# A searched order with new durations, constant products ahead of eight chunks, and loads held behind one matmul

## The chip, the cores and the metric

The kernel runs on one core of a Trainium2 chip. The metric is the device time of one execution in microseconds (us). The profile was taken of one further execution; its engines are named as on the page: PE (TensorE matmul), PEld (its weight loads), DVE (VectorE), ACT (ScalarE), POOL (GpSimd) and SP (SyncE, which here issues most DMAs).

## The reference

One block of a network on x of 2048 x 640 (all float32). A vector c gives six rows by silu(c) @ w_mod: sa, ca, ga, sb, cb, gb.

```python
x = A_u
h = layernorm(x) * (1 + ca) + sa
x = x + ga * A(h)          # S4D: a causal convolution along the sequence
h = layernorm(x) * (1 + cb) + sb
x = x + gb * B(h)          # SwiGLU: (silu(h @ w1) * (h @ w3)) @ w2

def A(u):                  # per channel d of 640, with N = 128 states
    P = exp((A * dt)[:, :, None] * arange(2048))
    K = 2 * einsum("dn,dnl->dl", C * dt, P).real
    return irfft(rfft(u, 4096) * rfft(K, 4096))[:2048] + u * D_skip
```

B has F = 1728 hidden channels.

## The kernel before

**Convolution.** The 640 channels are worked in five blocks (`NB`) of 128. For each block b three streams of work meet:

- *The kernel K* (`gen_tasks`, `gen_chunk`, from L566). Each block has 8 chunks of 16 channels, 40 in all. A chunk is: on POOL a phase table `ph` and three magnitude products (two into `yy`, one into `xx`); on ACT the sines into `tr`; on DVE five products into `yy` and `xx`; then on PE `product()` (L604): 32 small matmuls (128 x 32 by 128 x 64) that sum over the 128 states into `kps`, one half of a PSUM bank. ACT copies `kps` to `ks` (`rows`), and DVE adds the skip term (`skip`). `ph`, `xx`, `yy` and the halves of the bank `kg` are rings of two.
- *The normed input h* (`h_tasks`). Four quarters per block: load `xq` (for block 0 into `sp`), normalise into `hn` (`h_norm`, L990: four instructions of 128 x 128, on ACT or on DVE), multiply and add rows (`hn`, `hb`), store to DRAM `hs`, fetch as `xb`.
- *The spectra* (`first_tasks`, `spectra_tasks`). A transform in two steps: `ps` (PE, with the constant `wk`; from `xb` for h, from `ks` for K), copied into `sp` by ACT or DVE; then `fh` and `fk` (PE, with the constant `wb`), the complex product `fp` (DVE, from `hz` and `fk`), the first inverse step `fz` (PE, with the constant `wz`), copied to `zt` and stored to DRAM `zd`.

Before these, block 0 needs the parameters, the statistics of x (`xs`, `hscale`), and the modulation rows: `pm` (five groups of four products side by side, as the five pieces of `w_mod` land), `m`, `prow`, `rw`, `fold`; a second half of `w_mod` gives `cols`.

**What sets the order.** `Plan` (L172) lists all these tasks with an engine or a choice of engines, a duration, what each waits for, and the rings that it takes from and gives to. `place` walks through them, picks at each step the ready task by its start and its rank, and assigns the engine where there is a choice (`h_norm`, the copies of `ps` and `fz`, `al8`, `mag`). The ranks come from the long list `RANKS` (L33). The result is the program order on each engine (`Engines`, `InOrder`, L148: each instruction is ordered behind the one before it on its engine). All these instructions have L157 in the profile. SP's DMAs are in that order too; a DMA waits in SP until what it needs is there, and those behind it wait with it.

**Border.** When the last chunk of K and the last `hn` are done, `change` (L907) frees the tables and SP loads the first 512 rows of x (`x2[0]`), the constant `wd` (1 MB), and, as tasks, the first two weight tiles of the FFN and the first units of the second inverse step: `iz` (loaded from `zd`, without the last block's 128 columns) and `iy` (PE, with `wd`), which DVE adds to `x2`. After `plan.run()` (L946) the plan is over. Then come, written out in `run` (from L950): `izb` (L956), the last block's 128 columns of the first 512 rows, in four pieces of 128 KB (two issued by SP, two by ACT), which need the last `zd` store; `inverse` on them; `ln2` (L669: LayerNorm, `xn`, twenty transposes `tp` by PE, `v`, and the halves `xh` and `xl`); and the FFN. In this part the order on an engine is set by the scheduler and by priorities, and nothing but data holds a load back. Only `load_x2(1, last)` (L960) is given a wait for the last `izb` matmul.

**FFN.** `ffn` (L755) has four row blocks of 512 and 14 tiles of F. A tile is `up` (gu, L796 to L798, three matmuls per product since every factor is split into a high and a low half), `gate`, `down` (acc, L833). Tiles 0 and 13 of row block 0 were loaded and split ahead. While row block 0 runs, `mid` (L962) brings in the other 1536 rows' convolution: `inverse_unit(u)` for u = 2 to 7 loads `iz` (four pieces of 320 KB) and runs `iy` (L654); `load_x2(2)` and `load_x2(3)` load the rest of x. `x2[b]` is four loads of 320 KB. The first `iy` of the FFN (unit 2) stands on PE behind the first two tiles' gu.

Of the kernel before, what the change touches and what calls it, by code (L numbers as in the profile page):

```python
# [10 lines left out]
F32 = mybir.dt.float32  # L11
# [7 lines left out]
P = 128  # L19
# [263 lines left out]
class K:  # L283
# [282 lines left out]
    def gen_chunk(self, d0, tabs, off, E, place):  # L566
# [36 lines left out]

        def product():  # L604
            kps = place()
            for e in range(C // 4):
                for q in range(4):
                    i = e * 4 + q
                    for r in range(2):
# [938 lines left out]
```

## Time and profile before

| | |
|---|---|
| time, median of 3 | 1003.81 us (1002.39 to 1005.65) |
| profiled execution, its own time | 1003.62 us |
| its span | 1001.8 us |
| mean granted PE clock | 0.964 |
| busy: PE, DVE, ACT, POOL | 885.9, 667.6, 496.7, 287.4 us |
| moved by DMA | 122.03 MB, 122 GB/s on average |

The span reaches from the first to the last of the program's own instructions; the execution's time is 1.8 us longer. In the table of 40 slices, one slice is 25 us. PEclk is the clock that TensorE was granted, in tenths of full speed. A row of the timeline gives start and length of a run of like instructions on one engine, and in brackets how long the engine had been idle before it and what ended that. A float32 product is two records on PE, so x8 is four products. A row of busy time by stretch gives, after its length, busy us and number of instructions for PE, PEld, DVE, ACT and POOL, then the granted clock, the share of 16 DMA engines and GB/s. A row of a group by line gives busy time and mean ns, then idle time before it.

### The profile page before, as it was taken

How to read it: one execution, taken by the hardware profiler on the slowest of the kernel's cores; microseconds unless marked ns; L12 is line 12 of the kernel's file. 1: busy time of each engine (PE TensorE's matmuls, PEld its weight loads, DVE VectorE, ACT ScalarE, POOL GpSimd, SP SyncE). 2: the span in 40 equal slices, each digit the busy share in tenths (PEclk: the TensorE clock that was granted, in tenths of full speed). 3: DMA queues.
4: the chain of work that ended last, by engine and by line, in shares of the span. 5: the costliest groups of instructions: out<-in, count | busy, mean ns of one | idle time of the engine just before them, and what ended most of it. 6: DMA issues, size and time to landing. Idle time of an engine off the chain costs nothing.

```text
span 1001.8 us, 20149 instructions
## 1 busy us (share of the span) xinstructions
PE 885.9 (88%) x8073; PEld 706.8 (71%) x8073; DVE 667.6 (67%) x1234; ACT 496.7 (50%) x829; POOL 287.4 (29%) x293
## 2 busy tenths in 40 slices
PE   1464877889999992999999999999999999999997
PEld 1142766767887961677788888888888888888885
DVE  7998999999999573677664454463644544645442
ACT  6867787979787731432243242342333332433221
POOL 1798798989999230100000000000000000000000
PEclk9976998999999995999999999999999999999999
DMA  9954553624041398967132353233453323542301
GB/s 218 267 187 169 123 131 103 150 56 117 24 107 45 90 280 221 225 160 178 56 114 70 105 152 112 79 90 94 106 145 99 99 79 93 145 118 79 105 27 52
DMA packets 141189, 122.03 MB, mean 122 GB/s; under 512 B 13480, under 2 KB 124840, under 8 KB 139688
## 3 DMA queue, kind: packets, MB, share of 16 engines
q1 hardware_dynamic: 140360, 119.84, 44.5%
q8 instruction: 63, 1.03, 0.4%
q10 hardware_dynamic: 736, 0.92, 0.3%
q14 instruction: 30, 0.25, 0.1%
HBM read 99.75 MB, written 20.97 MB: 121 GB/s over the span
## 4 chain that ended last, share of the span: by engine, by line
PE 72%; DVE 13%; DMA 8%; ACT 3%; issue 3%; SPq 0%; ACTq 0%; DVEq 0%
PE acc L833 19%; PE gu L798 12%; PE gu L797 12%; PE gu L796 12%; PE ps L157 4%; DVE yy L157 3%; PE kps L157 2%; PE fk L157 2%; PE fz L157 2%; PE fh L157 2%; DVE xx L157 2%; DMA sp<-in_w_mod 2%; DVE fp L157 2%; DMA zd<-zt 2%; DVE hn L157 2%
## 5 line engine op out<-in xcount | busy, mean ns | idle before, releaser
L798 PE MATMUL gu<-xh,wl 128*128 128x512 f32 x540 | 212.9, 394 | 0.0
L797 PE MATMUL gu<-xl,wh 128*128 128x512 f32 x540 | 211.6, 392 | 0.0
L796 PE MATMUL gu<-xh,wh 128*128 128x512 f32 x540 | 210.7, 392 | 0.1
L732 ACT ACTIVATE wh<-wr 128x640 fp32r<-128x640 f32 x105 | 71.8, 731 | 136.0 <-PE gu L797 132.8
L744 POOL MEMSET w2l<- 64x640 f32 x3 | 1.9, 630 | 450.8 <-PE acc L833 450.8
L797 PEld LDWEIGHTS gu<-xl,wh 128*128 128x128 f32 x540 | 101.5, 188 | 23.6
L796 PEld LDWEIGHTS gu<-xh,wh 128*128 128x128 f32 x540 | 101.6, 188 | 22.8 <-ACT xh L666 0.5
L798 PEld LDWEIGHTS gu<-xh,wl 128*128 128x128 f32 x540 | 101.4, 188 | 21.4
L809 ACT ACTIVATE th<-gu 128x512 f32<-128x512 f32 x52 | 31.2, 599 | 130.7 <-PE gu L798 130.6
L811 DVE TENSOR_TENSOR a<-a,gu 128x512 f32<-128x512 f32 x52 | 35.7, 687 | 88.2 <-PE gu L798 88.1
L157 POOL TENSOR_TENSOR yy<-e,e 128x512 f32<-128x512 f32 x80 | 86.3, 1096 | 16.7 <-PE kps L157 11.9
L833 PE MATMUL acc<-w2l,ah 128*128 128x512 f32 x220 | 87.0, 396 | 0.0
L833 PE MATMUL acc<-w2h,ah 128*128 128x512 f32 x220 | 87.0, 395 | 0.0
L810 DVE SCALAR_TENSOR_TENSOR a<-th,gu 128x512 f32<-128x512 f32 x52 | 35.7, 687 | 76.5 <-ACT th L809 76.4
L733 ACT ACTIVATE w2h<-w2r 128x640 fp32r<-128x640 f32 x54 | 39.9, 738 | 94.2 <-issue 56.6
L745 DVE TENSOR_TENSOR w2l<-w2r,w2h 128x640 fp32r<-128x640 f32 (+1 forms) x54 | 44.4, 822 | 57.9 <-ACT w2h L733 57.8
L741 DVE TENSOR_TENSOR wl<-wr,wh 128x640 fp32r<-128x640 f32 x105 | 82.4, 818 | 0.0
L157 POOL TENSOR_TENSOR ph<-p,p 128x1024 int32<-128x1024 int32 x40 | 79.1, 1978 | 5.5 <-ACT tr L157 4.7
L833 PE MATMUL acc<-w2h,al 128*128 128x512 f32 x204 | 77.6, 395 | 0.0
L157 DVE TENSOR_TENSOR yy<-yy,tr 128x512 f32<-128x512 f32 (+1 forms) x80 | 75.4, 944 | 0.9 <-ACT tr L157 0.6
L157 PE MATMUL kps<-yy,xx 128*32 128x64 f32 x2560 | 51.5, 236 | 26.0 <-DVE xx L157 20.0
L157 PEld LDWEIGHTS kps<-yy,xx 128*32 128x32 f32 x2560 | 45.1, 117 | 35.9 <-issue 19.9
(229 smaller groups left out, 1688.0 us busy)
## 6 DMA issues: line engine op xcount, KB each, us to landing
wr<-in_w SPq DMA_DIRECT2D x104, 320.0 KB, 3.8
w2r<-in_w SPq DMA_DIRECT2D x52, 320.0 KB, 2.8
zd<-zt SPq DMA_DIRECT2D x39, 256.0 KB, 2.8
iz<-zd SPq DMA_DIRECT2D x24, 320.0 KB, 6.2
xs<-in_x SPq DMA_DIRECT2D x16, 320.0 KB, 11.4
hs<-hb SPq DMA_DIRECT2D x20, 256.0 KB, 2.4
xb<-hs SPq DMA_DIRECT2D x20, 256.0 KB, 4.4
x<-in_x SPq DMA_DIRECT2D x16, 320.0 KB, 5.6
```

The costliest lines, as they stand in the source:

```text
L157: self.prev = self.k.order(f(*a, **kw), self.prev)
L732: self.nc.scalar.activation(wh[:, i], raw[:, i], AF.Copy)
L733: self.nc.scalar.activation(w2h, w2r, AF.Copy)
L741: eng.tensor_tensor(wl[:, i], raw[:, i], wh[:, i].bitcast(F32), op=ALU.subtract)
L745: eng.tensor_tensor(w2l[q], w2r[q], w2h[q].bitcast(F32), op=ALU.subtract)
L796: nc.tensor.matmul(pg, wh[:, k, :], xh[:, k, :], start=(k == 0), stop=False)
L797: nc.tensor.matmul(pg, wh[:, k, :], xl[:, k, :], start=False, stop=False)
L798: nc.tensor.matmul(pg, wl[:, k, :], xh[:, k, :], start=False, stop=(k == KT - 1))
L809: nc.scalar.activation(th, gu[0], AF.Tanh, scale=0.5)
L810: nc.vector.scalar_tensor_tensor(a, th, 1.0, gu[0], op0=ALU.add, op1=ALU.mult)
L811: nc.vector.tensor_mul(a, a, gu[1])
L833: nc.tensor.matmul(acc[k], *two(a, w), start=(m == 0 and i == 0), stop=(m == 12 and i == 2))
```

## The change

Four things change.

1. The list `RANKS` is another one, and three durations and one wait that the plan reckons with are others: `h_norm` on DVE 1.75 instead of 0.85, `fold` 3.3 instead of 1.6, one more entry (400000 bytes) for the first loads, and in block 0 each `product` also waits for `wk`. So the order and the choice of engines of the whole convolution are new; it has the same tasks.
2. In block 0 each of the eight `product()` groups is preceded on PE by four products of the identity with the constant `wk` (128 x 256), into the same half bank, which the group then overwrites.
3. At the border, `awake` puts products of the identity with `wd` (128 x 512) into a bank that is not read: eight behind the last planned matmul, three behind the last `izb` matmul.
4. `held_back` makes every `load_x2` after the first and every `inverse_load` after `izb` wait for the last `izb` matmul.

The diff without the ranks:

```diff
         def product():
             kps = place()
+            if d0 < P:
+                for _ in range(4):
+                    nc.tensor.matmul(kps, self.ident, self.wk.rearrange("p a b -> p (a b)"), start=True, stop=True)
...
-    def load_x2(self, b, after=None):
+    def load_x2(self, b):
         for q in range(4):
-            i = self.nc.sync.dma_start(self.x2[b][q * 32:(q + 1) * 32], self.xv[q, :, 4 * b:4 * b + 4, :])
-            if after is not None:
-                self.tc.add_manual_dep(i.ins, after.ins.name, ...)
+            self.held_back(self.nc.sync.dma_start(self.x2[b][q * 32:(q + 1) * 32], self.xv[q, :, 4 * b:4 * b + 4, :]))
...
-                (other if g and other else self.nc.sync).dma_start(z[pr][g * 64:(g + 1) * 64], zv[:, t0:t0 + nj, d0:d1])
+                self.held_back((other if g and other else self.nc.sync).dma_start(z[pr][g * 64:(g + 1) * 64], zv[:, t0:t0 + nj, d0:d1]))
...
+    hold = None
...
         plan.run()
-        self.nc = nc = real
+        self.nc = real
...
-        z = self.inverse_load("izb", ip, "izb", 1, 0, 4, cut, D, nc.scalar)
-        last = self.inverse(0, 4, z, ps, "gu", 3, cut, D)
+        z = self.inverse_load("izb", ip, "izb", 1, 0, 4, cut, D, real.scalar)
+        self.awake(nc.tensor, po.tile([P, 512], F32, name="awake0", tag="acc4"), 8)
+        self.hold = nc.tensor.prev = self.inverse(0, 4, z, ps, "gu", 3, cut, D)
+        self.awake(nc.tensor, po.tile([P, 512], F32, name="awake1", tag="acc4"), 3)
...
-        self.load_x2(1, last)
+        self.load_x2(1)
...
-            add(n + "p", "PE", 1.1, lambda c=c: ch[c][4](), [n + f"m{i}" for i in range(5)], t + 3,
+            add(n + "p", "PE", 1.1, lambda c=c: ch[c][4](), [n + f"m{i}" for i in range(5)] + ([] if b else ["wk"]), t + 3,
...
-            add(n + "n", ("ACT", "DVE"), (1.95, .85), ...
+            add(n + "n", ("ACT", "DVE"), (1.95, 1.75), ...
...
-        add("ld", "SP", 0, None, [], next(lp), dma=[2560, 327680, 2560])
+        add("ld", "SP", 0, None, [], next(lp), dma=[2560, 327680, 2560, 400000])
...
-        add("fold", "DVE", 1.6, fold, ...
+        add("fold", "DVE", 3.3, fold, ...
...
+    def held_back(self, i):
+        if self.hold is not None:
+            self.tc.add_manual_dep(i.ins, self.hold.ins.name, mybir.DependencyInfo(mybir.DependencyClass.Sync, mybir.DependencyReason.DATA), reason="behind")
+
+    def awake(self, pe, to, n):
+        v = self.wd.rearrange("p a b c -> p (a b c)")[:, :512]
+        for i in range(n):
+            pe.matmul(to, self.ident, v, start=True, stop=True)
```

More of the change, by code (lines that the diff above doesn't have):

```diff
@@ L628, in pbank @@
         return self.psg.tile([P, 512], F32, name=name, tag="f", bufs=3)
-    def load_x2(self, b, after=None):
+    def load_x2(self, b):
         for q in range(4):
-            i = self.nc.sync.dma_start(self.x2[b][q * 32:(q + 1) * 32], self.xv[q, :, 4 * b:4 * b + 4, :])
-            if after is not None:
-                self.tc.add_manual_dep(i.ins, after.ins.name, mybir.DependencyInfo(mybir.DependencyClass.Sync, mybir.DependencyReason.DATA), reason="behind")
+            self.held_back(self.nc.sync.dma_start(self.x2[b][q * 32:(q + 1) * 32], self.xv[q, :, 4 * b:4 * b + 4, :]))
     def inverse_load(self, name, pool, tag, bufs, j0, nj, d0, d1, other=None):
@@ L1154, in h_tasks @@
             place = (lambda: self.pbank("hn")) if b else (lambda: self.psg.tile([P, 512], F32, name="hn", tag="f", bufs=3))
-            add(n + "n", ("ACT", "DVE"), (1.95, .85), lambda e, i=i, place=place: self.h_norm(b, i, place(), e), [n + "l", "hscale"], t, take=[(bank, 1)],
+            add(n + "n", ("ACT", "DVE"), (1.95, 1.75), lambda e, i=i, place=place: self.h_norm(b, i, place(), e), [n + "l", "hscale"], t, take=[(bank, 1)],
                 give=[("xq", n + "l")] if b else [])
@@ L1472, in fold @@
             V.tensor_mul(self.rB, self.rB, self.rows[2])
-        add("fold", "DVE", 1.6, fold, [f"rw{g}" for g in range(4)], 22, port=True)
+        add("fold", "DVE", 3.3, fold, [f"rw{g}" for g in range(4)], 22, port=True)
         add("wb", "SP", 0, lambda: nc.sync.dma_start(self.wb, self.t_wb), ["fold", "mr4", "lat1", "turn1"], 60, dma=[2097152])
```

130 rows, old and new, of the table RANKS are left out of this document.

## The prediction

> **What bounds the kernel now.** I read the page's slices first, then busy time by stretch of 25 us, then the stretch around 375 to 415 us by engine.
>
> ```profile
> span 1001.8 us, 20149 instructions
> ...
> PE   1464877889999992999999999999999999999997
> ...
> DVE  7998999999999573677664454463644544645442
> ...
> PEclk9976998999999995999999999999999999999999
> ```
>
> The right 24 slices are the FFN: PE is never idle there, at full clock. The left 15 are the convolution, where DVE is at nine tenths or more. Between them, in slice 16 (375 to 400 us), PE drops to 2 tenths and its clock to half. A gain can come from two places only: the convolution ends earlier, or the hole gets shorter. The FFN's instructions stay as they are, some 596 us from 405 to the end.
>
> ```profile
> core 0: us, PE busy (x) PEld busy (x) DVE busy (x) ACT busy (x) POOL busy (x), PEclk, DMA share, GB/s
> ...
> 50.00:75.00 25.00, 16.07 (x276) 10.07 (x280) 24.24 (x53) 17.26 (x36) 23.23 (x24) 0.77 0.55 185
> 75.00:100.00 25.00, 10.17 (x241) 6.53 (x232) 20.64 (x33) 19.85 (x31) 20.68 (x22) 0.69 0.49 170
> ...
> 275.00:300.00 25.00, 24.70 (x546) 21.12 (x544) 24.65 (x43) 22.31 (x40) 24.28 (x24) 1.00 0.45 108
> ...
> 325.00:350.00 25.00, 25.00 (x524) 22.39 (x522) 14.91 (x27) 17.87 (x32) 7.05 (x6) 1.00 0.34 85
> ```
>
> In the convolution DVE has almost no air (24.2 and 24.7 of 25), except in 75 to 100; POOL has 1 to 4 us in a stretch, ACT 3 to 8. From 275 on PE is full as well. So less DVE work helps early, and only as far as it lets PE do more before 275.
>
> The hole, on all engines:
>
> ```profile
> 375.38 1.94 PE L157 MATMUL iy<-iz,wd 128*64 128x512 f32 x8
> 386.66 1.54 PE L654 MATMUL iy<-izb,wd 128*64 128x128 f32 x6 [9.34 <-DMA izb<-zd]
> 392.12 1.94 PE L654 MATMUL iy<-izb,wd 128*64 128x128 f32 x10 [3.92 <-DMA izb<-zd]
> 399.41 4.53 PE L691 MATMUL tp<-ident,xn 128*128 128x128 f32 x20 [5.35 <-ACT xn L682]
> 404.04 1.20 PE L796 MATMUL gu<-xh,wh 128*128 128x512 f32 x3
> ```
>
> ```profile
> 383.25 1.25 SPq L644 DMA_DIRECT2D izb<-zd  x2
> 384.54 2.18 SPq L632 DMA_DIRECT2D x<-in_x  x4
> 386.78 0.48 SPq L644 DMA_DIRECT2D iz<-zd  x1
> 394.08 2.33 SPq L632 DMA_DIRECT2D x<-in_x  x4
> 396.46 4.96 SPq L644 DMA_DIRECT2D iz<-zd  x7
> ```
>
> ```profile
> 383.96 8.02 DMA izb<-zd
> ```
>
> ```profile
> DMA to landing us min/median/max: 2.8/4.6/8.0
> ```
>
> PE ends its planned work at 377.3. The last z store lands at 383.25, four izb pieces of 128 KB are issued (two by SP, two by ACT), and the last, issued by ACT at 383.96, takes 8.02 us, to 391.98: five loads of 320 KB were put into SP's queue right behind izb. Then come the matmuls, LayerNorm and twenty transposes, until gu starts at 404.04.
>
> **The change, part by part.** All against the profiled execution, 1003.62 us (span 1001.8 and 1.8 around it), 0.2 below the median 1003.81.
>
> *Loads held back.* In the built program of the changed kernel SP issues izb and then x21, x22, iz2, iz3, x23, the first of them waiting for the last izb matmul. Nothing runs beside izb any more. Its last piece then takes between 2.8 and 8.0 us; I take 4.0, near the median 4.6 and a little below, since that median holds pieces already in the crowd. 8.0 - 4.0 = **-4.0 us** (0 to -5.2).
>
> *The price of holding back.* iz2 was partly ahead (one piece at 386.78). Now, counted from the last izb matmul, it stands behind eight pieces of x21 and x22, and is the ninth to twelfth of 320 KB. The next weights stand behind x23, further from their use.
>
> ```profile
> 386.60:392.10 5.50, 1.54 (x6) 1.15 (x7) 0.00 (x0) 0.00 (x0) 0.00 (x0) 0.50 1.02 229
> ```
>
> ```profile
> 414.89 0.83 PE L654 MATMUL iy<-iz,wd 128*64 128x320 f32 x4
> ```
>
> At 229 GB/s a piece (327,680 bytes) takes 1.43 us, twelve 17.2; with some 2.3 us of latency (the quickest landing of 128 KB above, 2.8, less its own share of 0.6) the twelfth lands about 19.5 us behind. PE used iz2 414.89 - 394.06 = 20.8 us behind, and will want it 1.7 us sooner by the next term, at 19.1. I take **+0.7 us** (0 to +3); it is partly covered by the wait for the gate that stands behind those matmuls anyway.
>
> *Products of constants at the border.* Eight of 128x512 stand behind the last planned matmul, three behind the last izb matmul.
>
> ```profile
> 59.78 1.77 PE L157 MATMUL prow<-m,ident 128*128 128x512 f32 x4
> ...
> 73.05 1.96 PE L157 MATMUL kps<-yy,xx 128*32 128x64 f32 x64
> ...
> 79.35 1.16 PE L157 MATMUL kps<-yy,xx 128*32 128x64 f32 x64 [1.51 <-DVE xx L157]
> ```
>
> prow's two products (two records each) give 0.89 us for one at full clock. Eight take 7.1 us: from about 378.2, when ACT has emptied the bank, to 385.3, before izb lands (387.9). Three take 2.7 us, 5.3 at half clock, in the 5.35 us that PE waits for xn. So the products cost nothing as long as those two waits last; were both gone, 9.8 us. What they buy is the clock:
>
> ```profile
> 380.70:386.60 5.90, 0.00 (x0) 0.00 (x0) 0.00 (x0) 0.00 (x0) 0.00 (x0) 0.50 0.49 133
> ...
> 399.40:404.60 5.20, 5.09 (x21) 4.63 (x22) 2.31 (x4) 2.67 (x5) 0.00 (x0) 0.50 0.98 204
> 404.60:415.00 10.40, 10.37 (x47) 8.19 (x46) 3.89 (x6) 5.13 (x8) 2.60 (x2) 1.00 1.04 229
> ```
>
> ```profile
> 402.27 1.66 DVE L696 TENSOR_SCALAR v<-tp,cols 128x512 f32<-128x512 f32 x2 [2.76 <-PE tp L691]
> ```
>
> ```profile
> 398.43 1.73 ACT L682 ACTIVATE xn<-x,rs_n_n,rs_y_n 128x640 f32<-128x640 f32 x2 [20.24 <-DVE rs_n_n L337]
> ```
>
> ```profile
> 507.85 1.47 PE L691 MATMUL tp<-ident,xn 128*128 128x128 f32 x12
> ```
>
> At half clock a transpose takes 4.53/20 = 0.23 us, in the FFN 1.47/12 = 0.12. xn is ready at 400.16; the first v waits for its twelfth transpose until 402.27. At full clock it could start at about 400.5: **-1.7 us** (0 to -2.3, half of the 4.53).
>
> *The searched order.* The built programs differ in who does a job:
>
> ```profile
> L157 DVE TENSOR_SCALAR hn<-xq,rs_y_h,rs_n_h 128x128 f32<-128x128 f32 x44 | 18.2, 413 | 1.4 <-ACT sp L157 0.2
> ...
> L157 DVE COPY sp<-ps 128x512 f32<-128x512 f32 x19 | 12.7, 683 | 3.3 <-PE ps L157 3.1
> ```
>
> ```profile
> L157 ACT ACTIVATE sp<-ps 128x512 f32<-128x512 f32 x58 | 34.2, 595 | 12.0 <-PE ps L157 11.9
> ...
> L157 ACT ACTIVATE hn<-xq,rs_n_h,rs_y_h 128x128 f32<-128x128 f32 x20 | 9.2, 461 | 2.7 <-DMA xq<-in_x 1.8 <-DVE fp L157 0.4
> ```
>
> Twelve of the 44 hn go from DVE to ACT (12 x 0.413 = 5.0 us) and five sp copies (5 x 0.683 = 3.4); three small exchanges give 0.9 back. DVE loses 7.5 us, ACT gains 12 x 0.461 + 5 x 0.595 - 0.6 = 7.9, which its idle time takes. POOL's work stays within 1 us. Passed on in full, -7.5; with PE full from 275, perhaps nothing. I take half, **-3.7 us** (0 to -9, the end with PE's waits for iz0 at the tail).
>
> *Products in the first block.* Four products of 128x256 (0.44 us each at full clock, from prow; 1.8 a group, 3.6 at half) stand ahead of each of the first eight kps, and wait for the constant wk, which SP sends behind all of x and five loads of w_mod.
>
> ```profile
> 46.34 1.96 PE L157 MATMUL kps<-yy,xx 128*32 128x64 f32 x64
> ```
>
> ```profile
> 46.47 3.53 DMA sp<-in_x
> ```
>
> ```profile
> 49.00 2.10 POOL L157 TENSOR_TENSOR yy<-e,e 128x512 f32<-128x512 f32 x2
> ```
>
> The first kps, at 46.34, now stands behind the fifth pm and the first group. A load that SP issues behind both their loads landed at 50.0; pm (I reckon 1 to 2 us for four products side by side) and the group (1.8 to 3.6) put the first kps at about 54. Behind it on PE: prow, the second kps, ps. On POOL the third chunk's yy (49.00) waits for its buffer, to about 56, and DVE for that yy. POOL can bring forward 5 us of tables, and DVE statistics and the rsqrt, as the built order does. Its rows before that wait add up to 54, the product's copy by ACT is there at 55 to 58: 1 to 4 us idle. Later groups run while PE waits (16 of 25 and 10 of 25 us busy above). Against it stands the clock: kps 1.96 at half, 1.16 at full. I take **+1.5 us** (-3 to +14, the end if all eight groups at 1.8 us were on the path).
>
> Sum: -4.0 + 0.7 - 1.7 - 3.7 + 1.5 = -7.2; 1003.6 - 7.2 = **996.4 us**.
>
> **The rivals.** *Order pays in full*: -7.5 and 2 more at the tail, early stall 0: 1003.6 - 5.0 - 9.5 = 989. For it: DVE is the fullest engine up to 325. Against: PE is full from 275.
>
> *The clock falls anyway.* PE ended at 377.3 and the grant fell at 380.7, 3.4 us later; behind the eight products stand 2.6 us without work, behind the three about as much. If a pause of that size is enough, the transposes stay at 0.23 us and the first block's groups heat nothing, while their 1.5 stays: 1003.6 - 4.0 + 0.7 - 3.7 + 1.5 = 998. The Trainium skill (TensorE: Matmul & The Clock Gate, Part 1) speaks for this case in the first block: the window is about 3.4 us and runs freely, and one busy window is needed, which a group of four short products does not fill at full clock; its own example falls 5.2 us after the last matmul, later than the 3.4 here.
>
> *The gain is eaten at the border and the order gives nothing*: izb's last piece takes its median 4.6 (-3.4), iz2 is 3 late, the clock gives -1.7, the early stall costs 1.5: 1003.0, within 0.3%. In effect, the change doesn't do what it says.
>
> *Slower*: the first kps is 8 us later, and POOL's ring of two buffers hands that on. It decides if POOL's idle time, 6 us of 50 to 100, doesn't take the shift: then the whole convolution ends 8 us later plus half of the eight groups (7), less the border's 5: 1003.6 + 15 - 5 = 1013.6; half of it, 1008.
>
> **How the numbers follow.** Forecast 0.42 (own range 993 to 1000), order in full 0.13, clock falls 0.12, eaten 0.15, slower 0.18. About 0.3% (3 us) is what a measurement of this kernel can tell from no change: faster 0.67, same 0.15, slower 0.18. The range leaves out the lower half of "in full" and the upper half of "slower": 989 to 1008.
>
> **What would show it.**
>
> ```profile
> 344.98 1.75 SPq L157 DMA_DIRECT2D x<-in_x  x4
> ```
>
> Right: izb's slowest piece at 4 us instead of 8.02; PEclk 1.00 from 378 to 405; twenty transposes in 2.5 to 3 us; from the last izb matmul to gu 8.3 instead of 10.0; a wait for iz at the first iy of L656 under 2 us; the first load of the FFN's x, at 344.98, 2 to 3 us earlier; an idle DVE of 1 to 4 us at 54 to 58. The forecast is wrong if that load comes later than 348, or if DVE, relieved, is idle by as much as it was relieved.

## The result and the profile after

| | before | changed |
|---|---|---|
| device time, median | 1004.7 us (1002.39 to 1005.91, 4 runs) | 1041.9 us (1037.47 to 1042.57, 4 runs) |
| ratio to before, 95% interval | | 1.0368 (1.0345 to 1.0391) |
| profiled execution: time, span | 1003.62, 1001.8 | 1037.47, 1035.3 |

The change costs 37 us; forecast were 996.4 and a range of 989 to 1008. The profiled execution is the quickest of the four, 4.4 us under their median, so its trace accounts for 33.9 of the 37 us. The page of the changed kernel, its busy times and its slices (one is 25.9 us here):

```profile
PE 918.2 (89%) x8159; PEld 723.8 (70%) x8159; DVE 660.4 (64%) x1218; ACT 504.9 (49%) x845; POOL 287.4 (28%) x293
...
PE   2477667689989996799999999999999999999997
...
DVE  7977698959898954566765464464463464654442
...
PEclk9997887899999998999999999999999999999999
```

The FFN at the right looks as before. On the left DVE, which stood at nine tenths in eleven of the first thirteen slices, falls to 7, 7 and 6 tenths in slices 3 to 5 and to 5 in slice 9: less work and still more time. The hole at the border (slices 16 and 17 now, 6 and 7 tenths instead of 2) is shallower.

Two marks split the span: the end of PE's planned work (the last iy of L157) and the first gu of the FFN.

| us | before | changed |
|---|---|---|
| planned work ends | 377.3 | 417.8 |
| from there to the first gu | 26.7 | 19.5 |
| from the first gu to the end | 597.8 | 598.0 |

So the convolution is 40.5 us longer, the border 7.2 shorter, the FFN the same. The border first, PE's timeline and then DMA's and PE's waits in the changed kernel:

```profile
415.87 1.94 PE L157 MATMUL iy<-iz,wd 128*64 128x512 f32 x8
417.74 7.13 PE L157 MATMUL awake<-wd,ident 128*128 128x512 f32 x16
426.49 0.87 PE L656 MATMUL iy<-izb,wd 128*64 128x128 f32 x6 [1.62 <-DMA izb<-zd]
427.63 1.23 PE L656 MATMUL iy<-izb,wd 128*64 128x128 f32 x10 [0.28 <-DMA izb<-zd]
428.79 2.84 PE L157 MATMUL awake<-wd,ident 128*128 128x512 f32 x6
434.20 2.40 PE L695 MATMUL tp<-ident,xn 128*128 128x128 f32 x20 [2.57 <-ACT xn L686]
437.33 0.97 PE L800 MATMUL gu<-xh,wh 128*128 128x512 f32 x3 [0.73 <-ACT xh L670]
```

```profile
DMA to landing us min/median/max: 2.9/3.3/3.8
```

```profile
PE iy L656 <- DMA iz<-zd: 1.0, 1, 1.0
```

The slowest piece of izb takes 3.8 us instead of 8.02, the twenty transposes 2.40 instead of 4.53, and iz2 makes PE wait 1.0.

Now the convolution. Busy times by stretch, of the kernel before and then of the changed one (columns as in the prediction's table):

```profile
45.00:60.00 15.00, 11.82 (x229) 7.88 (x230) 14.83 (x28) 13.05 (x27) 14.54 (x17) 0.89 0.82 255
...
100.00:125.00 25.00, 21.09 (x420) 18.46 (x422) 23.42 (x47) 19.34 (x36) 19.26 (x19) 0.93 0.53 124
...
200.00:250.00 50.00, 43.28 (x894) 35.77 (x892) 47.33 (x88) 43.84 (x73) 43.36 (x41) 0.97 0.34 87
```

```profile
45.00:60.00 15.00, 13.23 (x102) 7.94 (x103) 12.55 (x30) 10.08 (x22) 14.40 (x16) 1.00 0.83 254
...
75.00:100.00 25.00, 18.71 (x288) 14.45 (x288) 17.64 (x31) 17.27 (x31) 20.64 (x20) 0.74 0.58 191
100.00:125.00 25.00, 16.15 (x239) 12.66 (x237) 15.19 (x28) 13.83 (x26) 15.88 (x17) 0.80 0.22 51
...
200.00:250.00 50.00, 42.93 (x774) 37.34 (x772) 36.80 (x69) 35.67 (x65) 26.25 (x27) 0.96 0.33 86
```

The early stretch, 45 to 60, loses 2.3 us of DVE's work, about what was forecast. The large losses come later: 8.2 us of DVE in 100 to 125 (the first hole), and 10.5 of DVE and 17.1 of POOL in 200 to 250 (the second). In 100 to 125 all four engines do less than before at once; none of them is the bound, they wait for each other. Waits between 45 and 380 us, before and changed (us in total, number of waits, longest one):

```profile
POOL yy L157 <- PE kps L157: 11.9, 11, 3.1
...
ACT ks L157 <- PE kps L157: 9.0, 14, 1.5
...
DVE ks L157 <- ACT ks L157: 4.5, 3, 2.8
```

```profile
POOL yy L157 <- PE kps L157: 38.9, 10, 17.3
DVE ks L157 <- ACT ks L157: 30.0, 10, 9.0
ACT ks L157 <- PE kps L157: 27.6, 16, 6.3
```

The one wait of 17.3 us shows how. From the timelines of the changed kernel around it, engine by engine:

```profile
204.81 1.17 PE L157 MATMUL kps<-yy,xx 128*32 128x64 f32 x64
209.34 2.30 PE L157 MATMUL ps<-wk,xb 128*64 128x128 f32 x32 [3.36 <-DVE hb L157]
...
219.11 6.43 PE L157 MATMUL ps<-wk,ks 128*64 128x128 f32 x96
...
232.95 1.17 PE L157 MATMUL kps<-yy,xx 128*32 128x64 f32 x64
...
225.60 0.60 ACT L157 ACTIVATE sp<-ps 128x512 f32<-128x512 f32 x1 [0.28 <-PE ps L157]
226.09 0.66 ACT L157 ACTIVATE ks<-kps 128x256 f32<-128x256 f32 x2
...
226.78 0.23 DVE L157 TENSOR_TENSOR ks<-kps,dsk 128x4 f32<-128x4 f32 x2 [9.04 <-ACT ks L157]
...
234.22 2.09 POOL L157 TENSOR_TENSOR yy<-e,e 128x512 f32<-128x512 f32 x2 [17.25 <-PE kps L157]
```

Read it backwards. POOL at 234.22 waits for a yy that PE's kps at 232.95 reads. That kps needs a half of the buffer kg, and both halves hold products of the new block (the second was made at 204.81), which ACT may copy into ks only when the old block's `ps<-wk,ks` have read it: the last six of these run from 219.11, behind ps that had waited for hb. So the copies come at 226.09, twenty us after the product, and in the order that the engines were given, six more groups of PE stand ahead of the kps. No engine is slow here; the order is.

### The profile page after: what moved, and what is told of

It is laid out like the page before. It is cut to its first block, busy times and chain, and to the rows that moved or that the text cites. A ratio compares the mean times of both kernels' runs of the same rounds, so it can differ in the third digit from the quotient of the medians.

```text
span 1035.3 us, 20303 instructions
## 1 busy us (share of the span) xinstructions
PE 918.2 (89%) x8159; PEld 723.8 (70%) x8159; DVE 660.4 (64%) x1218; ACT 504.9 (49%) x845; POOL 287.4 (28%) x293
## 4 chain that ended last, share of the span: by engine, by line
PE 69%; DVE 15%; DMA 4%; POOL 3%; issue 3%; ACT 3%; SPq 2%; ACTq 0%; DVEq 0%; POOLq 0%
PE acc L837 18%; PE gu L802 12%; PE gu L801 12%; PE gu L800 12%; PE ps L157 5%; DVE yy L157 4%; PE kps L157 3%; DVE fp L157 2%; PE fz L157 2%; DVE xx L157 2%; SPq L157 2%; DMA iz<-zd 2%; DVE hn L157 1%; PE iy L656 1%; PE fk L157 1%
## 5 line engine op out<-in xcount | busy, mean ns | idle before, releaser
L157 POOL TENSOR_TENSOR yy<-e,e 128x512 f32<-128x512 f32 x80 | 85.5, 1085 | 45.0 <-PE kps L157 38.9
L157 POOL TENSOR_TENSOR ph<-p,p 128x1024 int32<-128x1024 int32 x40 | 80.5, 2015 | 10.6 <-ACT tr L157 10.3
L157 DVE TENSOR_TENSOR yy<-yy,tr 128x512 f32<-128x512 f32 (+1 forms) x80 | 75.6, 946 | 3.1 <-ACT tr L157 2.5
L157 PE MATMUL kps<-yy,xx 128*32 128x64 f32 x2560 | 50.4, 232 | 23.4 <-DVE xx L157 21.9
L157 PEld LDWEIGHTS kps<-yy,xx 128*32 128x32 f32 x2560 | 43.9, 115 | 34.8 <-issue 10.6
```

Source lines behind the costliest of these rows:

```text
L157: self.prev = self.k.order(f(*a, **kw), self.prev)
```

## The experiments

Each ratio is to the kernel before and stands with its 95% interval. Of the terms, "the plan's end" needs a word. The list of ranks isn't itself an order: the plan places every task with its prices and waits, and takes the rank where several could go. So the kernel's own code gives a time for every task, without a run, and with it the end of PE's planned work: 363.0 us for the kernel before and 396.3 for the changed one.

**border_only.** Before, with held_back and awake alone.

```diff
+        self.awake(nc.tensor, po.tile([P, 512], F32, name="awake0", tag="acc4"), 8)
+        self.hold = nc.tensor.prev = self.inverse(0, 4, z, ps, "gu", 3, cut, D)
+        self.awake(nc.tensor, po.tile([P, 512], F32, name="awake1", tag="acc4"), 3)
```

> The kernel before with the edits of the border alone: the loads held back behind the last izb matmul and the eight and three products of constants; order, prices and first block are those of before. From the last planned matmul to the first gu the two traces show 26.7 us before (377.3 to 404.04) and 19.5 us after (417.8 to 437.33), and the FFN behind gu is as long in both. If the border does what it was meant to do by itself, this kernel is 7 us faster than before, 996 to 999. If those 7 us were only there because the late convolution left the queues empty (rival), it lies within 3 us of before.

999.0 us, ratio 0.9948 (0.9931 to 0.9965). From the end of the planned work to gu it has 19.2 us. The border gains 5.7 us by itself by the medians, 5.2 by the ratio.

**products_only.** Before, with the four products and the wait for wk in the plan.

```diff
+                for _ in range(4):
+                    nc.tensor.matmul(kps, self.ident, self.wk.rearrange("p a b -> p (a b)"), start=True, stop=True)
...
-            add(n + "p", ..., [n + f"m{i}" for i in range(5)], t + 3,
+            add(n + "p", ..., [n + f"m{i}" for i in range(5)] + ([] if b else ["wk"]), t + 3,
```

> The kernel before with the four products of constants ahead of each of the first eight kps, and the wait for wk that the plan needs for them; old ranks, old prices, old border. Theory of the products: they and the wait put the first block 8 to 11 us late and the order, worked off as written, hands that on and adds to it: 1015 to 1037. Theory of the order: the new ranks and prices are what loses, and the products cost what I had reckoned, 1 to 8 us: 1004 to 1012.

1027.5 us, ratio 1.0227 (1.0209 to 1.0245), as the theory of the products has it.

**no_products.** The changed kernel less the loop of four products.

> The changed kernel without the four products of constants in the first block; ranks, prices, the plan's wait for wk and the border stay, so every other instruction stands where it stood. Theory of the products: most of the 37 us comes back, 997 to 1010. Theory of the order: little comes back, 1025 to 1040, and the hole of DVE and POOL at 205 to 234 us is still there.

1032.2 us, ratio 1.0282 (1.0258 to 1.0306). Only 9.7 us come back, as the theory of the order has it. The second hole is still there: DVE does 38.75 us in 200 to 250, and POOL's longest wait for kps is 15.4.

**order_only.** Before, with the new list and the new prices.

```diff
-RANKS = (list of before)
+RANKS = (list of the changed kernel)
...
-            add(n + "n", ("ACT", "DVE"), (1.95, .85), ...
+            add(n + "n", ("ACT", "DVE"), (1.95, 1.75), ...
-        add("ld", "SP", 0, None, [], next(lp), dma=[2560, 327680, 2560])
+        add("ld", "SP", 0, None, [], next(lp), dma=[2560, 327680, 2560, 400000])
-        add("fold", "DVE", 1.6, fold, ...
+        add("fold", "DVE", 3.3, fold, ...
```

> The kernel before with the new list of ranks and the four new prices alone: no products, no wait for wk in the plan, old border. Since the wait is not there, the plan comes out a little otherwise than in the changed kernel. Theory of the order: 1020 to 1045. Theory of the products: 995 to 1008, as the forecast had it for the order (3.7 us gained) or a few us of loss.

1029.5 us, ratio 1.0244 (1.0226 to 1.0262). So each theory holds in the run that was made for it, and each had denied the loss of the other: the products with their wait cost 23 us on the old list, the new list without them costs 25. The two don't add up, since with both and the better border the change costs 37. What they may have in common is that the plan was given an input for which its list was not made; fold_price and wait_only, below, change one such input each.

**products_old_order.** Before, with the loop of products alone. The plan doesn't know of the wait, so the order is that of before.

> The kernel before with the four products of constants ahead of each of the first eight kps and nothing else: the plan does not know of the wait for wk, so every engine works in exactly the order of before. Theory of the lists (any other input to the plan throws the old list out of tune, and the loss lies in the order): the products cost only what they take themselves, as between the changed kernel and the one without products (planned end 417.8 against 411.9): 4 to 10 us more than before, 1008 to 1015. Theory of the products (their lateness is what the order multiplies): 15 to 25 us more, 1019 to 1030, as with the wait planned.

1016.3 us, ratio 1.0107 (1.0076 to 1.0138), some 11 us: just above the range of the lists and below that of the products. The first kps comes at 52.9 and the stretch from 45 to 60 shows whom that holds up (14.83 of DVE before):

```profile
45.00:60.00 15.00, 11.00 (x160) 7.73 (x160) 8.52 (x17) 7.16 (x15) 8.46 (x11) 0.69 0.84 251
```

**fold_price.** Before, with one number changed.

```diff
-        add("fold", "DVE", 1.6, fold, ...
+        add("fold", "DVE", 3.3, fold, ...
```

> The kernel before with one number changed: the plan reckons 3.3 instead of 1.6 us for fold. No instruction is added or taken away. Worked off with its own prices, the old list puts the last planned matmul of PE at 385.6 instead of 363.0. Theory of the lists: the chip follows the plan, 18 to 28 us slower than before, 1022 to 1032. Theory that a truer price makes a better or an equal order: within 3 us of before.

1030.0 us, ratio 1.0242 (1.0213 to 1.0272). One price, no instruction more or less: 24 us by the ratio. The theory of the lists had 18 to 28. (The new price of hn alone wasn't tried.) The new price moves jobs between engines as well as in time: 51 of the plan's tasks have another engine, and DVE is busy for 673.5 us instead of 667.6. Work alone isn't the cause, since in the changed kernel DVE has 7 us less than before.

**held_only** and **awake_only**, the two halves of the border; the edits are shown against border_only.

```diff
-        self.awake(nc.tensor, po.tile([P, 512], F32, name="awake0", tag="acc4"), 8)
...
-        self.awake(nc.tensor, po.tile([P, 512], F32, name="awake1", tag="acc4"), 3)
```

```diff
-        self.hold = nc.tensor.prev = self.inverse(0, 4, z, ps, "gu", 3, cut, D)
+        last = nc.tensor.prev = self.inverse(0, 4, z, ps, "gu", 3, cut, D)
...
+        self.hold = last
         self.load_x2(1)
+        self.hold = None
```

> The kernel before with the loads held back behind the last izb matmul, without the products at the border. Both edits of the border together gave 5.6 us. Forecast on record: the last piece of izb 4 us earlier, 0.7 lost on iz2: 3.3 faster, 1001. If the clock is what held the border up (rival), 1 us or less.

> The kernel before with the eight and three products of constants at the border, loads held back as little as before. Forecast on record: the transposes at full clock, 1.7 us faster, 1003. If the products work only where izb is not late, since a late izb lets the clock fall again before its matmuls (rival), nothing: 1004 to 1005.

held_only 999.3 us, 0.9949 (0.9925 to 0.9974); awake_only 1003.9 us, 0.9998 (0.9982 to 1.0014). The held loads give the border's gain, the products nothing that can be measured. PE's timeline of held_only and of awake_only:

```profile
386.24 3.10 PE L652 MATMUL iy<-izb,wd 128*64 128x128 f32 x16 [9.30 <-DMA izb<-zd]
394.69 4.19 PE L691 MATMUL tp<-ident,xn 128*128 128x128 f32 x20 [5.34 <-ACT xn L682]
```

```profile
389.12 0.87 PE L652 MATMUL iy<-izb,wd 128*64 128x128 f32 x6 [2.43 <-DMA izb<-zd]
393.78 1.94 PE L652 MATMUL iy<-izb,wd 128*64 128x128 f32 x10 [3.79 <-DMA izb<-zd]
395.65 3.69 PE L157 MATMUL awake<-wd,ident 128*128 128x512 f32 x6
401.07 2.40 PE L691 MATMUL tp<-ident,xn 128*128 128x128 f32 x20 [1.73 <-ACT xn L682]
```

Held back alone, izb's sixteen matmuls run in one stretch and the transposes stay slow. With the products alone the transposes take 2.40, but the late izb lets the clock fall in between (izb's last ten matmuls at 1.94, not 1.23). From the end of the planned work to gu that profile has 24.6 us, 2.1 less than before; but the planned work ended 2.3 us later, at 379.6, with the same instructions in the same order. So one profile shows a gain that ten executions don't, and it stays open.

**list_again.** The changed kernel with a list that I made by changing ranks at random and keeping what made the plan end earlier. All of its 1532 ranks differ from those of the changed kernel, so it is another list and not a correction of that one.

```diff
-RANKS = (list of the changed kernel, plan's end 396.3)
+RANKS = (list found for its prices and waits, plan's end 376.6)
```

> The changed kernel with another list of ranks: found by changing single ranks at random and keeping what made the plan, placed with the changed kernel's own prices and its wait for wk, end earlier. Everything else stays: prices, products in the first block, border. By its own reckoning this plan ends PE's work at 376.6 instead of 396.3 us. Theory of the lists (the list on hand fits neither the old prices nor the new; what is lost is the fit): about 20 us come back, 1016 to 1030. Rival, the truer prices and the wait for wk themselves: still 1036 to 1045.

1023.8 us, ratio 1.0191 (1.0172 to 1.0210): 18.1 us come back of 19.7 on paper.

**list_again_no_products.** The same less the loop of products.

> As the run before, and without the four products of constants in the first block. Theory of the lists: 20 us below the changed kernel without products (1032.2), 1006 to 1020. Rival: 1028 to 1036.

1022.4 us, ratio 1.0175 (1.0153 to 1.0196): above what I had expected, because the products cost only 1.4 us in this order, which the two intervals can't tell from nothing.

**list_old_prices.** border_only with a list found in the same way for the old prices.

> The kernel before with the border's edits and a list found in the same way for the old prices: the plan ends 2 us earlier than the one of before (361.1 against 363.0). If the plan's end tells the chip's to within 2 us, 997 (2 below the border alone, 999.0). If it tells it only to within some 7 us, as the runs so far have it (planned end to traced end differs by 14.3 in the kernel before, 15.6 without products, 16.9 with the price of fold, 29.4 with the list and prices alone), anywhere from 995 to 1015: a list that is 2 us better on paper is then no gain to count on.

1000.0 us, ratio 0.9954 (0.9937 to 0.9970), the same as border_only within the intervals. Two us less on paper are nothing to count on.

**products_later.** products_old_order with the products ahead of the third to the eighth kps only.

```diff
-            if d0 < P:
+            if 32 <= d0 < P:
```

> The kernel before in its own order with the four products of constants ahead of the third to the eighth kps only, so that the first two kps don't wait for wk. All eight cost 11 us (1016.3 against 1003.7 to 1005), and there the first kps came at 52.9 instead of 46.3. Theory of the wait: nearly all of the 11 us come from the late first kps; 1003 to 1008. Theory of the products' own time (3.8 us a group on a PE that is waited for): six eighths of it stay, 1010 to 1014.

1010.3 us, ratio 1.0060 (1.0037 to 1.0084): 6 of the 11 us stay, between the two theories. In the order of before about half is the late start and half the products' own time; the intervals leave each share wide.

**wk_early** and **one_ph.** The changed kernel with one rank changed: that of SP's load of wk, or that of POOL's phases of the first block's sixth chunk.

```diff
-(wk) -1276
+(wk) -1576
```

```diff
-(g0.5.ph) -1253
+(g0.5.ph) -1153
```

> The changed kernel with one rank changed, that of the load of wk (-1576 instead of -1276), so that SP sends it ahead of the loads of w_mod. The plan then has its first kps at 46.5 instead of 55.1 and its end at 375.5 instead of 396.3. Theory (the late first kps throws the order of the first block, and the list multiplies that): first kps below 50, no idle stretch of POOL above 6 us at 205 to 234, 1012 to 1026. Rival (the first kps is late for the products and for the loads ahead, whatever the rank): first kps above 52, 1034 to 1044.

> The changed kernel with one other rank changed, that of POOL's phases of the first block's sixth chunk (-1153 instead of -1253): the task comes later. wk stays late, and the plan's first kps stays at 55.1; its end goes to 376.2. Theory of the lists (any change that sets the order right again helps, with wk late or not): 20 us faster than the changed kernel, 1014 to 1028, and POOL's 17 us of waiting at 217 to 234 gone. Rival (the late wk is the cause by itself): within 6 us of 1041.9.

wk_early 1021.4 us, 1.0165 (1.0126 to 1.0204); one_ph 1023.8 us, 1.0194 (1.0165 to 1.0222). Either number gives back 18 to 20 us, as the plan's ends say (375.5 and 376.2). The first kps of wk_early came at 51.3, not below 50 as I had expected. The stretch of the second hole, wk_early and one_ph:

```profile
200.00:250.00 50.00, 42.63 (x837) 34.40 (x829) 46.59 (x86) 39.77 (x68) 37.84 (x38) 0.97 0.34 83
```

```profile
200.00:250.00 50.00, 42.70 (x846) 34.35 (x846) 46.64 (x86) 39.91 (x69) 37.78 (x39) 0.97 0.34 85
```

DVE does 46.6 us there instead of 36.8, POOL 37.8 instead of 26.3: the second hole is gone. The first one stays (DVE 17.4 and 16.1 us in 100 to 125, against 23.4 before). POOL's wait for kps falls to 18.2 and 20.5 us, its longest to 5.4 and 4.1:

```profile
POOL yy L157 <- PE kps L157: 18.2, 11, 5.4
```

```profile
POOL yy L157 <- PE kps L157: 20.5, 11, 4.1
```

So in the plan the late wk isn't the cause by itself: one_ph leaves it late there, at 55.1, and gains as much. On the chip the first kps of one_ph came at 50.2, earlier than the 53.8 of the changed kernel, so this pair doesn't settle it; another does. Without products the list of list_again has its first kps at 53.3 and takes 1022.4 us, the changed kernel's list has it at 52.5 and takes 1032.2. The late wk is one of several small shifts that decide which order comes out.

**wk_early_no_products.** wk_early less the loop of products.

> As wk_early without the four products of constants in the first block. If the products cost only by the wait for wk: within 3 us of wk_early. If they cost by their own time on PE: 5 to 9 us faster than wk_early.

1016.8 us, ratio 1.0126 (1.0099 to 1.0153): 4.7 us below wk_early, just short of the 5 to 9 expected if the products cost by their own time, and more than the 3 if they cost by the wait alone.

**wait_only.** Before, with the wait for wk in the plan and no product.

> The kernel before with the wait for wk put into the plan for the first eight kps, and nothing else: no product, no new price, old list. The plan's end goes from 363.0 to 380.6, its first kps from 43.7 to 53.4. With the products besides, 1027.5 was measured. Theory of the lists: most of those 23 us are there without any product, 1012 to 1024. Theory of the products: 1003 to 1008.

1023.1 us, ratio 1.0173 (1.0134 to 1.0211). Of the 23 us of products_only, 18 are the order that the plan makes of one more wait. POOL has one long wait for kps here too, 15.1 us, until 214.9.

The plan's end beside the traced one and the median, in us:

| kernel | plan's end | traced | median |
|---|---|---|---|
| list_old_prices | 361.1 | 381.3 | 1000.0 |
| before | 363.0 | 377.3 | 1004.7 |
| order_only | 375.0 | 404.4 | 1029.5 |
| wk_early | 375.5 | 397.8 | 1021.4 |
| wk_early_no_products | 375.5 | 399.5 | 1016.8 |
| one_ph | 376.2 | 405.1 | 1023.8 |
| list_again | 376.6 | 404.7 | 1023.8 |
| list_again_no_products | 376.6 | 405.2 | 1022.4 |
| wait_only | 380.6 | 401.9 | 1023.1 |
| products_only | 380.6 | 406.8 | 1027.5 |
| fold_price | 385.6 | 402.5 | 1030.0 |
| no_products | 396.3 | 411.9 | 1032.2 |
| changed | 396.3 | 417.8 | 1041.9 |

The traced end is that of the one profiled execution, and before, order_only, wait_only, products_only and fold_price have the old border, which is some 5 us slower. The plan tells a good order from a bad one (361 and 363 against all others), and within the changed kernel's family a gain of 20 us; it doesn't rank the lists between 375 and 386. The distance from plan to trace is 14 us in the kernel before and up to 29 elsewhere; why it varies so stays open.

## Why the prediction was wrong

The 37 us, step by step from before to changed: the border -5.7 (border_only against before), the new list with its prices and the planned wait +33.2 (no_products 1032.2 against border_only 999.0), the products +9.7 (changed 1041.9 against no_products). Sum +37.2; it must come out so, since each step starts where the last one ended, and another sequence would share the parts out otherwise.

*The searched order: -3.7, bounds 0 to -9.* This is the step that failed. The prediction took from the new order only who does a job: DVE relieved by 7.5 us. That came as reckoned: DVE's busy time fell by 7.2, from 667.6 to 660.4. But it let a job's place in its queue cost nothing and excluded a loss. Measured: +33.2, with the new prices and the planned wait in it. DVE lost 7 us of work, and its wait for ACT's copies of ks alone grew from 4.5 to 30.0 us. So both signs came that the prediction had named for being wrong: DVE, relieved, is idle by as much and more, and the first load of the FFN's x comes late:

```profile
373.20 2.31 SPq L157 DMA_DIRECT2D x<-in_x  x4
```

This load was to come before 348. The prediction's reading that DVE is at nine tenths or more in all fifteen slices of the convolution holds for eleven of them. The plan's own end, 396.3 against 363.0, said +33.3 without any run, and the prediction didn't use it (that it agrees to 0.1 us is luck: for order_only the plan said +12.0 and 25 were measured): by its own prices the changed kernel's list is worse than the old one. It is no better for the old inputs (385.3 with the old prices and no wait); of all sixteen mixtures of the three edited prices and the wait, its best is 373.3, with the new prices of hn and fold alone, and its worst is the one that was built.

*Products in the first block: +1.5, bounds -3 to +14.* The mechanism was right, the size wrong. First kps: about 54 forecast, 53.80 found, in PE's timeline of the changed kernel:

```profile
48.23 1.93 PE L157 MATMUL pm<-wb,sc 128*32 128x512 f32 x8 [1.14 <-DMA wb<-in_w_mod]
50.09 3.78 PE L157 MATMUL kps<-wk,ident 128*128 128x256 f32 x8
53.80 1.22 PE L157 MATMUL kps<-yy,xx 128*32 128x64 f32 x64
...
58.18 1.89 PE L157 MATMUL kps<-wk,ident 128*128 128x256 f32 x8
```

```profile
55.49 0.17 DVE L157 TENSOR_TENSOR ks<-kps,dsk 128x4 f32<-128x4 f32 x1 [1.39 <-ACT ks L157]
57.85 0.69 DVE L157 SCALAR_TENSOR_TENSOR yy<-yy,tr 128x512 f32<-128x512 f32 x1 [0.96 <-POOL yy L157]
```

DVE waits 2.4 us there, forecast 1 to 4. But the later groups aren't free, as assumed ("later groups run while PE waits"): they stand ahead of a kps for which ACT, DVE and POOL wait. The cost is 9.7 us in the changed kernel and 11 in the order of before, half of it there in the last six groups; behind wk_early it is 4.7 and in list_again 1.4. It goes by the order in which the same products stand. That a stall in an ordered pipeline adds up stood as the "slower" rival, at 8 to 15 us; that one was the nearest, and too small since it knew only the late start.

*Loads held back: -4.0, and +0.7 for iz2.* Right. Slowest piece of izb 3.8 us, forecast 4.0; iz2 made PE wait 1.0; held_only -4.4 us (-5.1 by the ratio) against -3.3 forecast.

*Products at the border: -1.7.* The transposes took 2.40 (forecast 2.5 to 3), 8.5 us lay between the last izb matmul and gu (forecast 8.3), yet awake_only gives nothing (-1.8 to +1.4 us, an interval in which the forecast -1.7 only just lies). The rival "the clock falls anyway" happened in border_only, whose stretches of 3.4 us show it:

```profile
391.20:394.60 3.40, 0.78 (x6) 0.58 (x6) 2.59 (x11) 1.55 (x2) 0.00 (x0) 1.00 0.95 204
394.60:398.00 3.40, 3.40 (x17) 3.02 (x15) 1.60 (x2) 1.40 (x4) 0.00 (x0) 0.50 1.07 226
```

The pause between the three products and the transposes filled one such stretch but for 0.78 us, and the next one ran at half clock: transposes 4.00 us. In the changed kernel the pause of 2.57 us was as long, and the clock stayed. Its clock had risen at 415.8; counted on from there in steps of 3.41 us (in border_only it fell at 394.62 and rose at 398.04), stretches begin at 429.4 and 432.8, so the pause from 431.63 to 434.20 fell into two of them, with about 2.2 and 2.0 us of work beside it (an estimate, from these starts and the rows above). The Trainium skill (TensorE: Matmul & The Clock Gate, Part 1) says that the window is about 3.4 us long and runs freely, and that the clock falls after an idle window; these two runs agree with the first, while the window of border_only wasn't idle. That the pause lay well here and badly there is chance. Whether the gain, where it comes, is worth the 1.5 us that one profile shows, the medians can't tell.

## What to carry to other kernels

Where engines work off a planned order, an edit to the plan's inputs is an edit to every queue: first compare when the plan itself starts each task before and after, and only then who does what. A list of ranks need not fit any other input than that for which it was found; one price, one wait or one rank moved this kernel by 18 to 26 us with no instruction added, so a new wait or a truer price needs a new search, and its result must beat the old plan's end before it is built. That isn't enough, as list_old_prices shows: 2 us on paper gave none. Gains that don't touch the plan can be had by themselves: holding back the loads behind izb gives 4 to 5 us (999.0 to 999.3, against 1004.7 and 1041.9), and no kernel here is faster.

## What the runs showed of the hardware

The clock's grant held in pieces of 3.4 us: a stretch of 3.4 us with 0.78 us of PE's work (391.2 to 394.6 in border_only) was followed by 3.4 us at 0.50, and in the changed kernel two with about 2.2 and 2.0 us (the estimate above) by full clock. The kernel before fits the same step: its clock fell at 380.7 and rose at 404.6, seven steps of 3.41 us. So the stretch need not be free of work to cost the clock. Four products of 128x256 took between 1.89 us (the changed kernel at 58.18, granted clock 1.00) and 3.78 (at 92.49, clock 0.50), and all thirty-two 22.5 us. The group at 50.09 took 3.78 as well, though the column of the clock has 1.00 in 45 to 60; pm, too, takes 1.93 there and 1.06 at 62.97, so the column doesn't show a slow clock so early in the span. All groups:

```profile
L157 PE MATMUL kps<-wk,ident 128*128 128x256 f32 x64 | 22.5, 512 | 1.2 <-DVE ks L157 1.2
```

Whether they warm the clock for their neighbours shows only between kernels of one order. From no_products to changed the granted clock went from 0.93 to 0.99 in 50 to 75, from 0.59 to 0.74 in 75 to 100 and from 0.86 to 0.80 in 100 to 125; from before to products_old_order it went from 0.69 to 0.77 and from 0.93 to 0.89 in the last two. So they raised it up to 100, one profile each, and the kernels were slower all the same.
